# Top-32 attention and capacity routing: the score mask as one comparison on GpSimd, a new order of VectorE's round, transposes issued together

## The chip, the cores and the metric

The kernel runs on one NeuronCore of a Trainium2 chip. Five engines work side by side, each through its own queue in order: TensorE (PE; its weight loads are shown as PEld), VectorE (DVE), ScalarE (ACT), GpSimd (POOL) and SyncE (SP), which issues the DMA transfers here. They wait for each other on semaphores. SBUF holds 128 rows (partitions); PSUM, which TensorE writes, has eight banks of 128 rows by 512 fp32 values. The metric is device time of one execution in microseconds (us); less is better.

## What is computed

Attention over 8 batches, 8 heads, 576 positions and 64 columns, in which each query keeps its 32 largest scores; then a mixture of experts, which routes each of the 4608 rows to its best expert, and in which each expert keeps its 80 rows with the largest gate.

```python
scores = scale * np.matmul(q, k.transpose(0, 1, 3, 2))
kth = np.partition(scores, -top_k, axis=-1)[..., -top_k:-top_k + 1]
mask = scores >= kth
scores = np.where(mask, scores, -1000000000.0)
scores = scores - np.max(scores, axis=-1, keepdims=True)
attn = np.exp(scores)
attn = attn / (np.sum(attn, axis=-1, keepdims=True) + 1e-09)
return np.matmul(attn, v).astype(np.float32)
...
logits = x @ w_gate
expert_idx = np.argmax(logits, axis=1)
...
keep = np.argpartition(-gw, capacity)[:capacity]
...
h = np.maximum(x[tok_idx] @ w1[e], 0.0)
out[tok_idx] = gate_w[tok_idx, None] * (h @ w2[e])
```

All inputs and the output are fp32.

## The kernel before, in words

The attention goes over 32 pairs of heads (`n`: batch and pair). A pair has 576 queries: four blocks of 128 rows and one of 64. In a full block each head is a *unit* of 128 queries by 576 keys; in the last block the 64 rows of both heads together are one unit. So a pair of heads has nine units (`UPP`), and the kernel 288 (`NU`). `run` writes the order out by hand: `step(i)` issues, for each unit, the pieces of work of several units that are in different stages. In the text a step is also called a round, and nine rounds a period; rounds are numbered 0 to 8 by the unit whose first maxima they take.

The stages:

- `load` (SP) brings q, k and v of a pair of heads, `turn` transposes q and k on TensorE into `sp`, a tile of four PSUM banks, of which there is one (`ps_s`), and ScalarE copies them into qT and kT.
- `front` multiplies scores of two units into the same `sp`; ScalarE copies them, scaled, to `s` (L195). A front is issued two rounds before its first unit.
- On VectorE, `parts` takes the eight largest of each of six pieces of a row (L202, "cand"); `search` finds the 24 largest of these by maxima and replacements (L213, L221); ScalarE compares all scores with the 24th and counts (`y`, L218, the sign); VectorE multiplies (L223), takes eight maxima of that (L225), and picks the threshold of the 32nd by the count (L228, `pick`, which writes `thr`).
- `drop` makes the unit's mask (L250): 0 or 1 for "below the threshold", plus the row's largest score, as bf16.
- `turn_w` makes the weights, transposed: TensorE multiplies the masks by `minus` (a diagonal of large negative numbers), which puts them transposed into PSUM (`ab` and `cc`, L268), and adds the transposed scores on top (L272). ScalarE takes the exponential (L275, L276) into `wT`. The `ab` tile has two PSUM banks; `cc` is one bank of a pool of two (`ps_c`).
- `back` multiplies `wT` by v into `cc` (L290), with a column of ones beside v that gives the sums; ScalarE copies the result to `xu` (L292).
- `norm` runs a few rounds behind, a piece a round: it divides by the sums (`z` on GpSimd, reciprocals on VectorE, `xn` on GpSimd, L307), stores `xn`, transposes it through `sp` (L318) into `xT`, and multiplies by the gate's weights (`lp`, L325, in the pool of `cc`); ScalarE copies that to `part` and GpSimd adds it to the logits `lg` (L334). Every two batches `gates` takes the row's best expert.

Three numbers set the order within a round: a letter is a piece of work on VectorE, `back` says how many units behind it works, and `G` is one of the six maxima of the new unit.

```python
back = dict(a=0, b=1, c=1, d=1, e=1, y=2, g=2, h=3, m=3)
for c in "GbGcGdGehGmyGga":
```

Here b to e are the replacements and maxima of `search`, y the multiplication, g the maxima of it, h the pick, m the mask, and a the first maximum over the candidates. After VectorE's letters a round issues `turn_w`, `front` or `turn`, `back` and the pieces of `norm`, each if its unit is due. Stores of zeros into the output (`clear`) and loads of the experts' weights are spread over the periods.

Behind the loop, `judge` checks that every threshold was found (if not, a slower exact path runs the attention again), and `finish` selects the rows of each expert and runs the experts.

## Time and profile before

| | |
|---|---|
| median of 3 runs | 1344.43 us (1344.4 to 1352.03) |
| the profiled execution | 1343.53 us |
| its span, from first to last instruction | 1341.7 us |
| granted TensorE clock, mean | 0.908 |
| VectorE busy | 84% of the span |
| TensorE busy | 81% |
| ScalarE busy | 51% |
| GpSimd busy | 7% |
| the attention loop, as the slices of the page show it | about 20 to 1175 us |

A row of a timeline has the start (us from the span's start), the length, the engine, the line, the operation, "out<-in", the shape and how many instructions are merged in it; in brackets stands how long the engine was idle just before, and what ended that. A row of a table of lines has the count behind an x, then the busy time in us, the mean of one in ns, and the idle time in front of these instructions with its releasers. A row of a table of stretches has the stretch, its length, the busy time and number of instructions of PE, PEld, DVE, ACT and POOL, then the granted clock, the share of the DMA engines and GB/s.

### The profile page before, as it was taken

Reading aid. Unit: us, or ns where it says so; the run is one execution under the profiler, and the core shown is the slowest. Engines: PE = TensorE matmul, PEld = TensorE weight load, DVE = VectorE, ACT = ScalarE, POOL = GpSimd, SP = SyncE. Lnnn points to the kernel's source line nnn. Section 1 sums busy time; section 2 is a strip of 40 time slices with the busy share of each in tenths; the row PEclk is TensorE's granted clock in tenths of the full one; section 3 lists DMA queues with packets and bytes.
Section 4 is the critical chain, followed back from the end, with each engine's and each line's share of the span. In section 5 each row is a group of like instructions: output and inputs, shape, how many; then the busy total and the mean of one; then the engine's idle time right before and its main releaser. Section 6 shows DMA issues by size and latency. Waiting matters only on the chain.

```text
span 1341.7 us, 38270 instructions
## 1 busy us (share of the span) xinstructions
PE 1081.9 (81%) x14862; PEld 834.7 (62%) x14862; DVE 1127.2 (84%) x5383; ACT 679.1 (51%) x1374; POOL 91.8 (7%) x213
## 2 busy tenths in 40 slices
PE   6888888888888888888888888888888888713987
PEld 3666666666666666666666666666666666603887
DVE  5999989999998999999999998999999999585001
ACT  4565555566555556565565556555555565300111
POOL 0000000000000000000000000000000000100111
PEclk9998989999889899898899989898898998855899
DMA  5033322222222122222222211111110110120660
GB/s 142 7 96 100 99 84 69 68 68 69 68 68 56 49 63 64 60 60 59 68 68 69 53 37 37 37 37 33 33 36 21 28 37 11 30 114 5 214 221 24
DMA packets 154590, 85.93 MB, mean 64 GB/s; under 512 B 118304, under 2 KB 136736, under 8 KB 154400
## 3 DMA queue, kind: packets, MB, share of 16 engines
q1 hardware_dynamic: 153376, 80.78, 21.0%
q0 software_dynamic: 1024, 2.62, 0.7%
q8 instruction: 118, 1.93, 0.6%
q14 instruction: 72, 0.59, 0.2%
HBM read 63.19 MB, written 20.19 MB: 62 GB/s over the span
## 4 chain that ended last, share of the span: by engine, by line
PE 47%; DVE 41%; ACT 8%; issue 2%; POOL 0%; DMA 0%; POOLq 0%; DVEq 0%; ACTq 0%
PE sp L190 11%; DVE cand L202 10%; PE ab L272 9%; DVE mask L250 8%; PE cc L290 7%; DVE y L223 6%; DVE w L225 6%; DVE cand L221 4%; PE ab L268 4%; ACT s L195 4%; PE yp L616 3%; PE cc L272 3%; DVE top L213 2%; PE cc L268 2%; PE sp L165 2%
## 5 line engine op out<-in xcount | busy, mean ns | idle before, releaser
L202 DVE MAX8 cand<-s 128x8 f32<-128x96 f32 x1728 | 432.0, 250 | 76.2 <-ACT s L195 76.2
L190 PE MATMUL sp<-kT,qT 64*128 64x288 f32 (+1 forms) x1280 | 233.0, 490 | 48.3 <-ACT s L195 25.7
L275 ACT ACTIVATE wT<-ab 128x1024 f32<-128x1024 f32 (+1 forms) x160 | 150.1, 938 | 236.6 <-PE ab L272 236.6
L290 PEld LDWEIGHTS cc<-vb,wT 128*64 128x64 f32 x4608 | 197.7, 153 | 62.2 <-issue 47.2
L218 ACT ACTIVATE y<-s,w 128x576 f32<-128x576 f32 x288 | 222.9, 774 | 20.2 <-DVE w L213 19.9
L290 PE MATMUL cc<-vb,wT 128*64 128x65 f32 x4608 | 227.2, 241 | 0.0
L195 ACT ACTIVATE s<-sp 128x1152 f32<-128x1152 f32 (+1 forms) x160 | 165.5, 1034 | 112.3 <-PE sp L190 108.0
L223 DVE TENSOR_TENSOR y<-s,y 128x576 f32<-128x576 f32 x288 | 216.6, 752 | 3.4 <-ACT y L218 1.4
L225 DVE MAX8 w<-y 128x8 f32<-128x576 f32 x288 | 214.0, 743 | 0.1
L268 PEld LDWEIGHTS <-mask 128*128 128x128 bf16 (+1 forms) x1600 | 106.2, 101 | 168.2 <-DVE mask L250 122.1
L268 PE MATMUL ab<-minus,mask 128*128 128x128 bf16 (+1 forms) x1280 | 120.1, 216 | 110.0 <-DVE mask L250 106.9
L272 PE MATMUL ab<-qT,kT 64*128 64x128 f32 (+1 forms) x2560 | 193.3, 293 | 0.0
L190 PEld LDWEIGHTS sp<-kT,qT 64*128 64x128 f32 (+1 forms) x1280 | 122.3, 204 | 106.1 <-ACT s L195 44.4
L272 PEld LDWEIGHTS ab<-qT,kT 64*128 64x128 f32 x2560 | 163.6, 196 | 10.0
L250 DVE TENSOR_SCALAR mask<-s,thr,top 128x576 bf16<-128x576 f32 x288 | 166.8, 579 | 1.5 <-DVE cand L202 0.6
L213 DVE MAX8 top<-cand 128x8 f32<-128x48 f32 x576 | 111.3, 193 | 0.1
L221 DVE MATCH_REPLACE8 cand<-top,cand 128x48 f32<-128x48 f32 x576 | 111.3, 193 | 0.0
L290 PE MATMUL cc<-vr,wT 128*64 128x65 f32 x1152 | 97.5, 235 | 0.0
L268 PE MATMUL cc<-minus,mask 128*64 128x128 bf16 (+1 forms) x320 | 76.3, 238 | 0.0
L292 ACT COPY xu<-cc 128x130 f32<-128x130 f32 (+1 forms) x160 | 42.2, 264 | 64.7 <-PE cc L290 64.7
L290 PEld LDWEIGHTS cc<-vr,wT 128*64 128x64 f32 x1152 | 70.4, 151 | 0.0
L272 PE MATMUL cc<-qT,kT 64*64 64x128 f32 (+1 forms) x640 | 69.6, 297 | 0.0
(165 smaller groups left out, 996.1 us busy)
## 6 DMA issues: line engine op xcount, KB each, us to landing
w<-in_moe_w_dram SPq DMA_DIRECT2D x32, 512.0 KB, 4.7
w<-in_moe_w_dram SPq DMA_DIRECT2D x8, 2048.0 KB, 12.9
out_dram<-zero SPq DMA_DIRECT2D x9, 1024.0 KB, 8.2
qn<-in_q_dram SPq DMA_DIRECT2D x64, 128.0 KB, 2.7
kn<-in_k_dram SPq DMA_DIRECT2D x64, 128.0 KB, 2.7
vb<-in_v_dram SPq DMA_DIRECT2D x64, 128.0 KB, 2.4
xd<-xn SPq DMA_DIRECT2D x32, 256.0 KB, 2.4
qn<-in_q_dram SPq DMA_DIRECT2D x32, 32.0 KB, 2.8
```

Source lines behind the costliest of these rows:

```text
L190: nc.tensor.matmul(o, lhsT=qT[d, t * P : t * P + m], rhs=kT[d, j * HS : (j + 1) * HS], start=True, stop=True)
L195: nc.scalar.activation(s[:, : g * S].rearrange("p (j c) -> p j c", c=HS), ps[:, : 2 * g, :HS], Act.Copy, scale=TINY)
L202: nc.vector.max(out=cand[:, j, :], in_=s[:, j * S // NG : (j + 1) * S // NG])
L218: nc.scalar.activation(y, s, Act.Sign, bias=w9[:, 7:8], scale=-1.0, accum_out=cnt)
L221: nc.vector.match_replace(out=cand, in_to_replace=dst, in_values=cand, imm_value=LOW)
L223: nc.vector.tensor_tensor(out=y, in0=s, in1=y, op=Alu.mult)
L225: nc.vector.max(out=w9[:, 8:], in_=y)
L250: nc.vector.tensor_scalar(self.mask[i], s, self.thr[:, i : i + 1], top[:, 0, 0:1], op0=Alu.is_lt, op1=Alu.add)
L268: nc.tensor.matmul(dst[h][c], lhsT=masks[h][:, keys[c]], rhs=eye[h], start=c in (0, NF), stop=False, skip_group_check=True)
L272: nc.tensor.matmul(dst[h][c], lhsT=kT[heads[h], keys[c]], rhs=qT[heads[h], rows], start=False, stop=True, skip_group_check=True)
L275: nc.scalar.activation(wT[:, : 2 * NF, :m], ab.rearrange("p h c r -> p (h c) r")[:, :, :m], Act.Exp, scale=scale)
L290: nc.tensor.matmul(cc[r : r + TL, o], lhsT=wT[:, h * NF + c if c < NF else 2 * NF, r : r + TL], rhs=vb[:, c, h, :] if c < NF else vr[:, h, ...
```

## The change

The mask becomes one comparison, s below thr, without the row's largest score added, and moves from VectorE to GpSimd (`below`). The exponentials then are taken without subtracting the largest score; `z`, the sums, are kept for all pairs in one tile, and `judge` also asks that none of them is below 1e-30. The lean path keeps `drop`.

The round is written anew: the pick of a unit and its mask come a round later than before and stand at the round's start; y stands at its end; `turn_w` and `back` come one round later, so the loop drains in five rounds.

`turn` issues all ten transposes of q and k before the first of ScalarE's two copies. `norm` transposes `xn` into two tiles of the small pool of `cc`, of which the second also takes the product with the gate's weights; that product is done in column halves of 64. The tile of zeros shrinks to 128 columns, and the stores of zeros take rows of 512 bytes from it.

```diff
-    zero = const.tile([P, Dm], F32, name="zero")
+    zero = const.tile([P, P], F32, name="zero")
...
+            self.z = vpool.tile([P, 1 if lean else NP, NK, 2], F32, name="z")
+            nc.gpsimd.memset(self.z, 1.0)
...
-            for j, (src, name) in enumerate(zip(self.qk.pop(n), ("qT", "kT"))):
-                t = self.qkp.tile([P, S], F32, name=name, tag=name)
-                ps = four[:, 2 * j : 2 * j + 2, :].rearrange("p j c -> p (j c)")
-                self.turn_in(ps, src.rearrange("p c h d -> p c (h d)"))
-                nc.scalar.copy(t, ps[:, :S])
-                ts_.append(t)
-            self.turned[n] = ts_
+            ps = [four[:, 2 * j : 2 * j + 2, :].rearrange("p j c -> p (j c)") for j in range(2)]
+            for j, src in enumerate(self.qk.pop(n)):
+                self.turn_in(ps[j], src.rearrange("p c h d -> p c (h d)"))
+            self.turned[n] = [self.qkp.tile([P, S], F32, name=name, tag=name) for name in ("qT", "kT")]
+            for j in range(2):
+                nc.scalar.copy(self.turned[n][j], ps[j][:, :S])
...
-            self.drop(i)
-            yield
+
+        def below(self, i):
+
+            self.top.pop(i)
+            self.mask[i] = self.rows.tile([P, S], BF16, name="mask", tag="mask", bufs=3)
+            nc.gpsimd.tensor_scalar(self.mask[i], self.s.pop(i), self.thr[:, i : i + 1], None, op0=Alu.is_lt)
...
-            while self.fronts:
-                yield
-            ps = self.four()[:, :2, :].rearrange("p j c -> p (j c)")
-            self.turn_in(ps, xn)
+
+            ps, rest = (self.ps_c.tile([P, 512], F32, name="xp", tag="cc") for _ in range(2))
+            for c in range(NF):
+                nc.tensor.transpose(ps[:, c * P : (c + 1) * P], xn[:, c, :], ident)
+            nc.tensor.transpose(rest[:, :TL], xn[:TL, NF, :], ident[:TL, :TL])
             xT = self.xT
-            nc.scalar.copy(xT[:, :S], ps[:, :S])
-            yield
-            ps = self.ps_c.tile([P, 512], F32, name="lp", tag="cc")
-            lp = ps[:, : NK * E].rearrange("p (c e) -> p c e", e=E)
+            nc.scalar.copy(xT[:, : NF * P], ps)
+            nc.scalar.copy(xT[:, NF * P : S], rest[:, :TL])
+            yield
+            lp = rest[:, P : P + NK * E].rearrange("p (c e) -> p c e", e=E)
             for c in range(NK):
-                nc.tensor.matmul(lp[:, c, :], lhsT=xT[:, c * P : (c + 1) * P], rhs=wg[:, hp, :], start=True, stop=True)
+                for r in range(0, P, TL):
+                    nc.tensor.matmul(lp[r : r + TL, c, :], lhsT=xT[:, c * P + r : c * P + r + TL], rhs=wg[:, hp, :],
+                                     start=True, stop=True)
...
-                back = dict(a=0, b=1, c=1, d=1, e=1, y=2, g=2, h=3, m=3)
-                for c in "GbGcGdGehGmyGga":
+                back = dict(a=0, b=1, c=1, d=1, e=1, y=2, g=3, h=4, m=4)
+                for c in "GhmbGcGdGeGGgay":
...
+                    elif c == "m":
+                        if 0 <= i - back[c] < NU:
+                            self.below(i - back[c])
...
-                j = i - 3
+                j = i - 4
...
-                j = i - 4
+                j = i - 5
```

What it does to the order, at three places. Line numbers of the changed kernel run a few higher than those of the kernel before (L202 becomes L204, L213 L215, L221 L223, L223 L225, L225 L227, L228 L230, L268 L274, L290 L296). First VectorE, one round before, from the maximum of the candidates to the maximum of y:

```order
L213 MAX w_6463<-cand 128x8
L228 SCALAR_TENSOR_TENSOR pick,thr<-past,cnt,w_6338 128x9
L202 MAX cand<-s 128x8
L250 TENSOR_SCALAR mask<-s,thr,top 128x576
L223 TENSOR_TENSOR y<-s,y 128x576
L202 MAX cand<-s 128x8
L225 MAX w_6387<-y 128x8
```

And in the changed kernel, the end of one round and the start of the next:

```order
L215 MAX w_6758<-cand 128x8
L204 MAX cand<-s 128x8 x2
L227 MAX w_6645<-y 128x8
L215 MAX top<-cand 128x8
L225 TENSOR_TENSOR y<-s,y 128x576
L204 MAX cand<-s 128x8
L230 SCALAR_TENSOR_TENSOR pick,thr<-past,cnt,w_6645 128x9
```

The mask is gone from VectorE; y stands last in its round, a whole round ahead of the maximum that reads it, and the pick second in the next.

Second GpSimd's queue over one period, before:

```order
L301 TENSOR_SCALAR z<-xu 128x8
L301 TENSOR_SCALAR z<-xu 64x2
L307 TENSOR_TENSOR xn<-xu,z 128x512
L307 TENSOR_TENSOR xn<-xu,z 64x128
L334 TENSOR_TENSOR lg<-lg,part 128x40
```

And in the changed kernel:

```order
L307 TENSOR_SCALAR z<-xu 128x8
L307 TENSOR_SCALAR z<-xu 64x2
L238 TENSOR_SCALAR mask<-s,thr 128x576 x2
L313 TENSOR_TENSOR xn<-xu,z 128x512
L313 TENSOR_TENSOR xn<-xu,z 64x128
L238 TENSOR_SCALAR mask<-s,thr 128x576 x3
L343 TENSOR_TENSOR lg<-lg,part 128x40
L238 TENSOR_SCALAR mask<-s,thr 128x576 x4
```

Nine masks now stand among the pieces of `norm`; the addition to `lg`, which reads what ScalarE copied of TensorE's product, stands between the masks of rounds 1 and 2.

Third TensorE around the transposes of `xn`, with the engines that an instruction waits for, before:

```order
L165 MATMUL sp<-ident,xn 128x128 [waits Activation_49,Pool_49]
L165 MATMUL sp<-ident,xn 128x128 x3
L166 MATMUL sp<-ident,xn 128x64 [waits Pool_49]
L190 MATMUL sp<-kT,qT 128x288 [waits Activation_49]
L190 MATMUL sp<-kT,qT 128x288 x3
L290 MATMUL cc<-vb_128,wT 64x65 x8
```

And in the changed kernel:

```order
L192 MATMUL sp<-kT,qT 128x288 [waits Activation_49]
L192 MATMUL sp<-kT,qT 128x288 x3
L324 MATMUL xp<-ident,xn 128x128 [waits Activation_49]
L324 MATMUL xp<-ident,xn 128x128 x3
L325 MATMUL xp<-ident,xn 128x64 [waits Activation_49]
L296 MATMUL cc<-vb_130,wT 64x65 x8
L296 MATMUL cc<-vr_131,wT 64x65 x2
```

The front no longer stands behind these transposes, but the back does, and the last transpose has a wait of its own for ScalarE: one of the two small buffers still holds the `cc` of the back behind it, so the second tile takes the place of the first.

More of the change, by code (lines that the diff above doesn't have):

```diff
@@ L20 @@
 LOW = -3.0e38
+FAR = 1e-30
 TINY = 2.0 ** -48
@@ L109, in clear @@
         return [lambda i=i: nc.sync.dma_start(
-            out[i : i + r, :].rearrange("(p r) d -> p r d", p=P),
-            zero.unsqueeze(1).to_broadcast([P, r // P, Dm])) for i in range(0, N, r)]
+            out[i : i + r, :].rearrange("(p r) (c d) -> p (r c) d", p=P, d=P),
+            zero.unsqueeze(1).to_broadcast([P, r * Dm // P // P, P])) for i in range(0, N, r)]
     class Attention:
@@ L168, in turn @@
         def turn(self, n):
-            ts_ = []
             four = self.four()
-            for j, (src, name) in enumerate(zip(self.qk.pop(n), ("qT", "kT"))):
-                t = self.qkp.tile([P, S], F32, name=name, tag=name)
-                ps = four[:, 2 * j : 2 * j + 2, :].rearrange("p j c -> p (j c)")
-                self.turn_in(ps, src.rearrange("p c h d -> p c (h d)"))
-                nc.scalar.copy(t, ps[:, :S])
-                ts_.append(t)
-            self.turned[n] = ts_
+            ps = [four[:, 2 * j : 2 * j + 2, :].rearrange("p j c -> p (j c)") for j in range(2)]
[4 more added lines that the diff above has]
+                nc.scalar.copy(self.turned[n][j], ps[j][:, :S])
         def front(self, n, t):
@@ L248, in drop @@
             s, top = self.s.pop(i), self.top.pop(i)
-            self.mask[i] = self.rows.tile([P, S], BF16, name="mask", tag="mask", bufs=3)
+            self.mask[i] = self.rows.tile([P, S], BF16, name="mask", tag="mask", bufs=2)
             nc.vector.tensor_scalar(self.mask[i], s, self.thr[:, i : i + 1], top[:, 0, 0:1], op0=Alu.is_lt, op1=Alu.add)
@@ L298, in norm @@
             parts = ((slice(0, P), slice(0, NF)), (slice(0, TL), slice(NF, NK)))
-            z = self.small.tile([P, NK, 2], F32, name="z", tag="z")
+            z = self.z[:, n % NP if not self.lean else 0]
             for p, cs in parts:
@@ L430, in run @@
                 i = 0
-                while i < NU + 4 or later:
+                while i < NU + 5 or later:
                     step(i)
@@ L438, in judge @@
             small = self.small
-            least = small.tile([P, 1], F32, name="least", bufs=1)
-            nc.vector.tensor_reduce(least, self.thr, axis=AX, op=Alu.min)
+            least = small.tile([P, 2], F32, name="least", bufs=1)
+            nc.vector.tensor_reduce(least[:, 0:1], self.thr, axis=AX, op=Alu.min)
+            nc.vector.tensor_reduce(least[:, 1:2], self.z.rearrange("p n c h -> p (n c h)"), axis=AX, op=Alu.min)
+            nc.vector.tensor_scalar(least[:, 1:2], least[:, 1:2], -FAR, None, op0=Alu.add)
+            nc.vector.tensor_tensor(out=least[:, 0:1], in0=least[:, 0:1], in1=least[:, 1:2], op=Alu.min)
             ps = self.ps_c.tile([P, 512], F32, name="tp", tag="cc")
-            nc.tensor.transpose(ps[:1, :P], least, ident)
+            nc.tensor.transpose(ps[:1, :P], least[:, 0:1], ident)
             low = small.tile([1, 1], F32, name="low", bufs=1)
```

## The prediction

> **What bounds the kernel now.** I read the page's busy times first, then the chain that ended last, then the stretch from 200 to 1100 us, where the attention loop runs undisturbed, by lines, and at last the timeline of one pair of heads.
>
> ```profile
> PE 1081.9 (81%) x14862; PEld 834.7 (62%) x14862; DVE 1127.2 (84%) x5383; ACT 679.1 (51%) x1374; POOL 91.8 (7%) x213
> ...
> PE 47%; DVE 41%; ACT 8%; issue 2%; POOL 0%; DMA 0%; POOLq 0%; DVEq 0%; ACTq 0%
> ...
> 200.00:1100.00 900.00, 758.80 (x9906) 573.80 (x9902) 835.10 (x4134) 522.59 (x1058) 56.37 (x131) 0.93 0.20 53
> ...
> L202 DVE MAX8 cand<-s 128x8 f32<-128x96 f32 x1354 | 338.9, 250 | 55.8 <-ACT s L195 55.8
> ...
> L250 DVE TENSOR_SCALAR mask<-s,thr,top 128x576 bf16<-128x576 f32 x225 | 130.3, 579 | 0.6 <-PE ab L272 0.3 <-DVE cand L202 0.3
> ```
>
> VectorE is busy for 835 of these 900 us, and almost all of its rest (55.8) is waiting for fresh scores s. The chain nevertheless runs through TensorE for 47%: the loop is one in which VectorE makes masks, TensorE turns them into weights and, behind them in its queue, makes the scores that VectorE needs next. 225 masks in 900 us are 4.0 us a unit, and a pair of heads is nine units: 36.0 us a period, 32 periods.
>
> **VectorE's part.** One unit's round on VectorE, from one first maximum to the next:
>
> ```profile
> 605.73 0.24 DVE L202 MAX8 cand<-s 128x8 f32<-128x96 f32 x1
> ...
> 606.94 0.21 DVE L228 SCALAR_TENSOR_TENSOR pick<-past,cnt,w 128x9 f32<-128x9 f32 x1
> 607.07 0.08 DVE L228 DVE_READ_ACCUMULATOR pick<-past,cnt,w 128x1 f32 x1
> ...
> 607.26 0.58 DVE L250 TENSOR_SCALAR mask<-s,thr,top 128x576 bf16<-128x576 f32 x1
> 607.76 0.75 DVE L223 TENSOR_TENSOR y<-s,y 128x576 f32<-128x576 f32 x1
> 608.43 0.26 DVE L202 MAX8 cand<-s 128x8 f32<-128x96 f32 x1
> ...
> 609.37 0.24 DVE L202 MAX8 cand<-s 128x8 f32<-128x96 f32 x1
> ```
>
> A round without waits is 609.37 - 605.73 = 3.64 us. The mask holds the queue for 607.76 - 607.26 = 0.50 us, so the new round is 3.14 us: 28.3 us for nine instead of 32.8. If VectorE alone counted, this would be 4.5 us a period. It doesn't, so the rest of the loop has to be walked through.
>
> **The mask on GpSimd.** No row shows this form there. The nearest:
>
> ```profile
> L307 POOL TENSOR_TENSOR xn<-xu,z 128x512 f32<-128x512 f32 x32 | 33.4, 1043 | 89.2 <-DVE z L304 84.6 <-PE cc L290 4.5
> ...
> L334 POOL TENSOR_TENSOR lg<-lg,part 128x40 f32<-128x40 f32 x24 | 8.6, 360 | 403.6 <-ACT part L333 403.6
> ...
> L74 POOL MEMSET R<- 128x640 f32 x1 | 0.6, 621 | 0.0
> ```
>
> From below: a memset of 640 takes 0.62, so 576 elements 0.56 us, without reading anything. From above: the product of 512 with two inputs grows by (1043 - 360) / 472 = 1.45 ns an element, so 576 take 1.14 us. I take 1.0, by the product, the nearest row of arithmetic on a full tile, less a little for its second input. In the new round the pick stands second, so it ends 0.37 us into the round; with about 0.13 us to start, the mask is ready 1.5 us into it. At 607.84 it was ready 2.1 us into the old, longer round. The Trainium skill (GPSIMD Engine Reference, its opening) speaks against the move: it calls this engine the wrong one for ordinary elementwise arithmetic, VectorE being about twice as fast. Twice the 579 ns would be 1.16 us, and the sum by it about 1225; no row here shows the move itself.
>
> **TensorE's part, and ScalarE's behind it.** Durations as start to start, at full clock but for the three rows from 623 to 628:
>
> ```profile
> 604.26 0.40 PE L268 MATMUL ab<-minus,mask 128*128 128x128 bf16 x4 [1.58 <-DVE mask L250]
> ...
> 606.12 1.14 PE L190 MATMUL sp<-kT,qT 64*64 64x288 f32 x8
> 608.01 1.24 PE L190 MATMUL sp<-kT,qT 64*128 64x288 f32 x8 [0.75 <-ACT s L195]
> 609.18 0.69 PE L290 MATMUL cc<-vb,wT 128*64 128x65 f32 x16
> ...
> 610.50 0.40 PE L268 MATMUL ab<-minus,mask 128*128 128x128 bf16 x4
> ...
> 613.50 0.66 PE L165 MATMUL sp<-ident,xn 128*128 128x128 f32 x4
> ...
> 617.58 1.28 PE L325 MATMUL lp<-wg,xT 128*128 128x8 f32 x10
> 618.72 0.38 PE L268 MATMUL ab<-minus,mask 128*128 128x128 bf16 x4
> ...
> 622.90 0.29 PE L268 MATMUL ab<-minus,mask 128*128 128x64 bf16 x4 [1.67 <-DVE mask L250]
> ...
> 623.65 1.97 PE L272 MATMUL ab<-qT,kT 64*128 64x64 f32 x16
> ...
> 625.96 2.29 PE L190 MATMUL sp<-kT,qT 64*128 64x288 f32 x8
> ...
> 632.39 0.66 PE L165 MATMUL sp<-ident,kn 128*128 128x128 f32 x4 [1.03 <-ACT qT L176]
> ...
> 633.17 0.68 PE L290 MATMUL cc<-vb,wT 128*64 128x65 f32 x8
> ...
> 634.49 0.40 PE L268 MATMUL ab<-minus,mask 128*128 128x128 bf16 x4
> ...
> 636.95 1.24 PE L190 MATMUL sp<-kT,qT 64*128 64x288 f32 x8
> ```
>
> ```profile
> 609.29 1.13 ACT L195 ACTIVATE s<-sp 128x1152 f32<-128x1152 f32 x1 [0.59 <-PE sp L190]
> ...
> 610.77 0.78 ACT L218 ACTIVATE y<-s,w 128x576 f32<-128x576 f32 x1
> ...
> 613.25 1.02 ACT L275 ACTIVATE wT<-ab 128x1024 f32<-128x1024 f32 x1 [1.61 <-PE ab L272]
> 614.18 0.27 ACT L276 ACTIVATE wT<-cc 128x128 f32<-128x128 f32 x1
> 614.40 0.64 ACT L320 COPY xT<-sp 128x576 f32<-128x576 f32 x1
> ```
>
> So a whole turn_w takes 2.46 (634.49 to 636.95), and 1.86 from its second mask on (604.26 to 606.12); a front 1.17 (608.01 to 609.18), the short one 1.14; a back 1.32 (609.18 to 610.50; the short one too, 633.17 to 634.49); the short turn_w 0.75 and then 2.31 at half clock, 1.15 at full; one set of transposes about 0.8 (632.39 to 633.17); lp 1.14 (617.58 to 618.72). On ScalarE the exponentials take 1.15 (613.25 to 614.40) and s 1.13.
>
> What the other edits do here. The transposes of q and k lose the 1.03 us in which TensorE stood for the copy of q, once a period. The wait for the copies then falls on the next front, which a back now stands in front of. The transposes of xn no longer hold the large buffer, but the second small one comes free only when ScalarE has copied the first, so the fifth transpose, and the back queued behind it, waits for that copy, and the copy for s. lp becomes twice as many products of half the columns: from below 20 passes at back's 1.32 / 40 each, 0.66; from above 2.28, as many passes again at the old price. I take 0.7, since back's halves are the same kind.
>
> **One period, walked through** (us from the start of round 0, in which the third pair of the head before is turned):
> - Mask ready 1.5; second half of turn_w 3.4; front 4.55; exponentials 4.55 and s 5.7, in time for round 2 at 6.28. Four transposes 5.15; ScalarE's copy, after s, 6.3; last transpose 6.5; back 7.8; lp 8.5; ScalarE's part 8.75.
> - Now GpSimd's queue: lg stands in it ahead of round 2's mask. Its input comes at 8.75, it ends at 9.25, and the mask, whose pick was done at 6.65, is ready only at 10.3.
> - Second half of turn_w 12.2; front 13.35; s 14.5. Round 4 was due at 12.56: VectorE stands 1.95 us.
> - Short turn_w 15.25; transposes of q and k 16.9; the two copies 18.2, back beside them 18.2; front 19.4; s 20.6, due 14.5 + 6.28 = 20.8.
> - Short back 20.7; turn_w 23.2; short front 24.3; back 25.6; turn_w 28.1; front 29.25; s 30.45, due 14.5 + 15.7 = 30.2.
>
> The period is 30.45 us where lg is issued (three of four periods). Without lg, round 2's turn_w starts when lp ends, at 8.5, and s comes at 13.35: 29.25. Mean 30.15. The old period holds 36.0 - 32.8 (nine rounds) - 2.2 (55.8 of waiting for s in 25 periods) = 1.0 us of reciprocals, gates and short waits; I add half of that, 0.5, since some of it falls where VectorE waits for s.
>
> **The clock.** One thing is left:
>
> ```profile
> 620.10:623.50 3.40, 1.73 (x28) 1.23 (x26) 3.37 (x20) 2.01 (x4) 0.00 (x0) 1.00 0.00 0
> 623.50:626.90 3.40, 3.40 (x27) 2.97 (x27) 3.33 (x21) 0.71 (x2) 0.30 (x1) 0.51 0.00 0
> ```
>
> After a stretch in which TensorE was busy for half the time, it is granted half the clock. The mean of 0.93 says that this holds for 14% of the time, 5 us a period. In the new loop TensorE is on the path nearly throughout, so the same 5 us would cost 2.5; but its gaps are shorter (1.2 for the xn copy, 1.1 for the late mask). I take half, 1.25, between 0 and 2.5.
>
> **The sum.** 30.15 + 0.5 + 1.25 = 31.9 us, 4.1 less than 36.0; times 32, 131 us. At the end come a fifth step of draining and three small VectorE instructions, some 2.5 us. The zero fill in 512-byte rows costs nothing: DMA's share is 0.20, and nobody waits for these stores. From the profiled execution's 1343.53 us (span 1341.7), which is within 0.1% of the median 1344.43: 1343.5 - 131 + 2.5 = 1215 us.
>
> The ends: no half clock, -40; mask 0.56, twice in a period on the path, -28: 1147. Full half clock +40; mask 1.14, +9; ScalarE's queue (a sign of 0.78 us ahead of s or wT) and port conflicts, 1 us a period, +32: 1296.
>
> **Sharing between VectorE and GpSimd.**
>
> ```profile
> 1141.34 1.39 POOL L307 TENSOR_TENSOR xn<-xu,z 128x512 f32<-128x512 f32 x2 [4.46 <-PE cc L290]
> ...
> 1142.08 0.25 DVE L202 MAX8 cand<-s 128x8 f32<-128x96 f32 x1
> ...
> 1142.36 0.39 DVE L228 SCALAR_TENSOR_TENSOR pick<-past,cnt,w 128x9 f32<-128x9 f32 x1
> ```
>
> Here a pick, which has two inputs, took 0.39 instead of 0.21 and ended when GpSimd's xn ended (1142.73); a one-input maximum beside the same xn kept its 0.25. A mask at 0.5 to 1.5 of a round lies beside one-input work; y comes at 2.45. The Trainium skill (SBUF — State Buffer, "Who interferes with whom") has the rule for it: VectorE's two-input instructions and a GpSimd instruction that reads exclude each other wholly. The row agrees. By it the late mask of round 2 holds the pick of round 3 by up to 0.9 us, which the wait for s at round 4 covers.
>
> **Rivals.**
> - VectorE alone bounds (buffers hide all of the walk): 28.3 + 0.5 = 28.8, 7.2 us less a period, about 1115. Against it stand lg in GpSimd's queue and the copy in the middle of the transposes. 0.07.
> - TensorE and ScalarE give back more (half clock as before, y in front of s): 34.3 us a period, about 1290 and up to 1330. 0.17.
> - No effect, because the walk, not VectorE, already set the period: within 1%, 1344. Against it: VectorE was busy for 93% of the loop, so what it loses can't all have been slack. 0.05.
> - Slower: a GpSimd mask of m us ends at 0.5 + m; past m = 1.95 it holds y, and the round is 0.5 + m + 0.67. It decides from 4.0, m = 2.85. At m = 3.2 it is 4.37 a unit, 39.3 a period, 32 x 3.3 = 106 more: 1450. Only a compare three times as dear as xn's product does this. 0.05.
>
> Forecast 0.66. Range 1160 to 1285. About 1% is what a measurement of this kernel tells from no change: faster by more 0.90, within 0.05, slower 0.05.
>
> **What would show it.** Right: VectorE without L250, rounds of 3.14; masks on POOL near 1.0 us; POOL's lg waiting on ScalarE with the mask behind it, VectorE idle for s about 2 us a period in front of round 4; TensorE's fifth xn transpose waiting for xT; no TensorE wait for qT. Wrong: masks past 1.2 us, y or picks lengthened in most rounds, a granted clock well under 0.9 in the loop, or a period under 30.

## The result, and the profile after

| | before | after |
|---|---|---|
| median of 4 runs | 1345.61 us (1344.4 to 1352.03) | 1307.79 us (1299.17 to 1308.85) |
| ratio, with its 95% interval | 1 | 0.970 (0.964 to 0.975) |
| profiled execution's span | 1341.7 us | 1307.1 us |
| granted TensorE clock, mean | 0.908 | 0.900 |

The change gains 38 us. The forecast was 1215 us, a gain of 129; its range ended at 1285. The direction was right, the size was not. One of the four runs of the kernel with the old transposes, below, was in a slow state, 1346.43 us, and is not counted.

The page of the changed kernel, first the busy times, then the chain that ended last, then four groups of instructions (count, busy us, mean ns, and the idle time in front with its releaser):

```profile
PE 1064.4 (81%) x15182; PEld 816.9 (62%) x15182; DVE 1000.7 (77%) x5098; ACT 676.6 (52%) x1406; POOL 612.1 (47%) x502
...
DVE 43%; PE 34%; POOL 9%; issue 7%; ACT 5%; DMA 0%; SPq 0%; POOLq 0%; ACTq 0%; DVEq 0%
...
L238 POOL TENSOR_SCALAR mask<-s,thr 128x576 bf16<-128x576 f32 x288 | 495.8, 1723 | 394.9 <-DVE cand L223 386.8
L204 DVE MAX8 cand<-s 128x8 f32<-128x96 f32 x1728 | 399.1, 245 | 163.2 <-ACT s L197 162.9
...
L225 DVE TENSOR_TENSOR y<-s,y 128x576 f32<-128x576 f32 x288 | 236.0, 819 | 7.6 <-ACT y L220 7.6
...
L274 PE MATMUL ab<-minus,mask 128*128 128x128 bf16 (+1 forms) x1280 | 125.4, 223 | 128.3 <-POOL mask L238 127.7
```

The same two waits in the kernel before:

```profile
L202 DVE MAX8 cand<-s 128x8 f32<-128x96 f32 x1728 | 432.0, 250 | 76.2 <-ACT s L195 76.2
...
L268 PE MATMUL ab<-minus,mask 128*128 128x128 bf16 (+1 forms) x1280 | 120.1, 216 | 110.0 <-DVE mask L250 106.9
```

VectorE lost its masks: it is busy for 127 us less. Most of that came back as waiting. It now waits 162.9 us for scores (76.2 before), and TensorE stands 127.7 us in front of products that read a mask (106.9 before). One mask takes 1.723 us on GpSimd, where the forecast had 1.0. POOL, which was not on the chain before, is 9% of it.

How long a period is can be read from GpSimd, which makes one xn for each pair of heads. Its timeline in the kernel before, the first and the last xn:

```profile
64.60 1.39 POOL L307 TENSOR_TENSOR xn<-xu,z 128x512 f32<-128x512 f32 x2 [2.50 <-DVE z L304]
...
1167.56 1.39 POOL L307 TENSOR_TENSOR xn<-xu,z 128x512 f32<-128x512 f32 x2
```

And in the changed kernel, with the masks and the addition to lg of one period between:

```profile
64.97 1.91 POOL L313 TENSOR_TENSOR xn<-xu,z 128x512 f32<-128x512 f32 x2
...
656.60 1.91 POOL L313 TENSOR_TENSOR xn<-xu,z 128x512 f32<-128x512 f32 x2
...
661.88 1.72 POOL L238 TENSOR_SCALAR mask<-s,thr 128x576 bf16<-128x576 f32 x1 [1.39 <-DVE cand L223]
...
671.07 0.39 POOL L343 TENSOR_TENSOR lg<-lg,part 128x40 f32<-128x40 f32 x1 [4.35 <-ACT part L342]
671.45 3.42 POOL L238 TENSOR_SCALAR mask<-s,thr 128x576 bf16<-128x576 f32 x2
...
1136.13 1.39 POOL L313 TENSOR_TENSOR xn<-xu,z 128x512 f32<-128x512 f32 x2
```

Between first and last lie 31 periods: 1102.96 / 31 = 35.58 us before, 1071.16 / 31 = 34.55 us after. The period shrank by 1.0 us; the forecast had it shrink by 4.1, from 36.0 to 31.9. (The last period drains and is shorter, so the means lie a little under the undisturbed stretch.) Before the first xn and behind the last the kernels differ by 3 us together, so the loop holds nearly all of the gain, and all of what is missing.

The 31 periods are not alike. By the starts of xn, the eight without an addition to lg took 30.8 to 33.2 us, 31.7 on average; those with it, leaving out the draining last one, took 32.9 to 40.3, 36.0 on average. The walk's sum gave 31.0 (29.25 + 0.5 + 1.25) and 32.2: without lg it was nearly right, and what is missing lies in the periods with lg.

One period with lg, from round 0 at 661.30, on VectorE's timeline:

```profile
656.78 1.48 DVE L225 TENSOR_TENSOR y<-s,y 128x576 f32<-128x576 f32 x1
...
661.30 0.25 DVE L204 MAX8 cand<-s 128x8 f32<-128x96 f32 x1
661.47 0.21 DVE L230 SCALAR_TENSOR_TENSOR pick<-past,cnt,w 128x9 f32<-128x9 f32 x1
...
664.42 0.25 DVE L204 MAX8 cand<-s 128x8 f32<-128x96 f32 x1
...
668.31 0.21 DVE L230 SCALAR_TENSOR_TENSOR pick<-past,cnt,w 128x9 f32<-128x9 f32 x1
...
673.73 0.77 DVE L225 TENSOR_TENSOR y<-s,y 128x576 f32<-128x576 f32 x1
...
680.12 0.26 DVE L204 MAX8 cand<-s 128x8 f32<-128x96 f32 x1 [5.62 <-ACT s L197]
...
696.93 0.25 DVE L204 MAX8 cand<-s 128x8 f32<-128x96 f32 x1
```

The period is 696.93 - 661.30 = 35.63 us, and one wait in it, 5.62 us in front of round 4, is most of the lost time. Followed back: round 2's pick ended at 668.52, but its mask ran only from 671.45 to 673.17, behind lg, which began at 671.07. The same stretch on TensorE:

```profile
668.63 0.27 PE L325 MATMUL xp<-ident,xn 64*128 64x64 f32 x1 [1.18 <-ACT xT L327]
...
670.04 0.71 PE L333 MATMUL xp<-wg,xT 128*64 128x8 f32 x20
670.68 0.40 PE L274 MATMUL ab<-minus,mask 128*128 128x128 bf16 x4
...
673.22 0.51 PE L274 MATMUL ab<-minus,mask 128*128 128x128 bf16 x4 [1.97 <-POOL mask L238]
...
676.53 2.29 PE L192 MATMUL sp<-kT,qT 64*128 64x288 f32 x8
```

TensorE stood 1.97 us between its first and its second mask. The front behind it, which makes the scores that VectorE waits for, began at 676.53 and took 2.29 us; at full clock it takes 1.24. The table of stretches (PE, PEld, DVE, ACT, POOL busy, then the granted clock) shows why:

```profile
669.95:673.36 3.41, 1.44 (x38) 1.18 (x34) 3.41 (x18) 1.23 (x4) 2.29 (x3) 1.00 0.29 113
673.36:676.78 3.42, 3.42 (x27) 2.55 (x27) 1.13 (x3) 0.75 (x1) 1.50 (x1) 0.50 0.02 5
676.78:680.19 3.41, 3.41 (x22) 2.07 (x24) 0.07 (x1) 1.68 (x4) 0.00 (x0) 0.50 0.00 0
```

In the stretch of the stand TensorE was busy for 1.44 of 3.41 us, 42%, and for the next two stretches it was granted half the clock, just where the path runs through it. A stand as long in round 0 of the same period, 1.95 us up to 663.66, lay across two stretches, which were still busy for 59% and 84%, and the clock stayed at 1.00 behind both.

### The profile page after: what moved, and what is told of

It is laid out like the page before. It is cut to its first block, busy times and chain, and to the rows that moved or that the text cites. A ratio compares the mean times of both kernels' runs of the same rounds, so it can differ in the third digit from the quotient of the medians.

```text
span 1307.1 us, 38981 instructions
## 1 busy us (share of the span) xinstructions
PE 1064.4 (81%) x15182; PEld 816.9 (62%) x15182; DVE 1000.7 (77%) x5098; ACT 676.6 (52%) x1406; POOL 612.1 (47%) x502
## 4 chain that ended last, share of the span: by engine, by line
DVE 43%; PE 34%; POOL 9%; issue 7%; ACT 5%; DMA 0%; SPq 0%; POOLq 0%; ACTq 0%; DVEq 0%
DVE cand L204 12%; DVE y L225 9%; POOL mask L238 8%; DVE w L227 7%; PE ab L278 7%; PE sp L192 7%; DVE cand L223 5%; ACT s L197 4%; PE cc L296 3%; PE yp L631 3%; PE ab L274 3%; DVE top L215 3%; PE cc L278 2%; DVE pick L230 2%; DVE top L506 1%
## 5 line engine op out<-in xcount | busy, mean ns | idle before, releaser
L238 POOL TENSOR_SCALAR mask<-s,thr 128x576 bf16<-128x576 f32 x288 | 495.8, 1723 | 394.9 <-DVE cand L223 386.8
L204 DVE MAX8 cand<-s 128x8 f32<-128x96 f32 x1728 | 399.1, 245 | 163.2 <-ACT s L197 162.9
L225 DVE TENSOR_TENSOR y<-s,y 128x576 f32<-128x576 f32 x288 | 236.0, 819 | 7.6 <-ACT y L220 7.6
L274 PEld LDWEIGHTS <-mask 128*128 128x128 bf16 (+1 forms) x1600 | 106.4, 102 | 200.8 <-POOL mask L238 140.5
L274 PE MATMUL ab<-minus,mask 128*128 128x128 bf16 (+1 forms) x1280 | 125.4, 223 | 128.3 <-POOL mask L238 127.7
L192 PE MATMUL sp<-kT,qT 64*128 64x288 f32 (+1 forms) x1280 | 223.1, 473 | 5.0 <-ACT kT L180 2.5
L278 PE MATMUL ab<-qT,kT 64*128 64x128 f32 (+1 forms) x2560 | 213.2, 314 | 0.0
L227 DVE MAX8 w<-y 128x8 f32<-128x576 f32 x288 | 213.1, 740 | 0.0
L296 PEld LDWEIGHTS cc<-vb,wT 128*64 128x64 f32 x4608 | 180.0, 141 | 45.9 <-ACT wT L282 26.7
L296 PE MATMUL cc<-vb,wT 128*64 128x65 f32 x4608 | 207.7, 228 | 0.9 <-ACT wT L282 0.9
L278 PEld LDWEIGHTS ab<-qT,kT 64*128 64x128 f32 x2560 | 180.7, 214 | 11.0
L215 DVE MAX8 top<-cand 128x8 f32<-128x48 f32 x576 | 109.5, 190 | 0.1
L223 DVE MATCH_REPLACE8 cand<-top,cand 128x48 f32<-128x48 f32 x576 | 109.4, 190 | 0.0
L296 PE MATMUL cc<-vr,wT 128*64 128x65 f32 x1152 | 92.8, 225 | 0.0
L274 PE MATMUL cc<-minus,mask 128*64 128x128 bf16 (+1 forms) x320 | 78.3, 245 | 0.0
L278 PE MATMUL cc<-qT,kT 64*64 64x128 f32 (+1 forms) x640 | 75.7, 319 | 0.0
L296 PEld LDWEIGHTS cc<-vr,wT 128*64 128x64 f32 x1152 | 65.6, 141 | 0.0
L343 POOL TENSOR_TENSOR lg<-lg,part 128x40 f32<-128x40 f32 x24 | 9.2, 383 | 113.5 <-ACT part L342 113.5
```

The source lines that it names most:

```text
L192: nc.tensor.matmul(o, lhsT=qT[d, t * P : t * P + m], rhs=kT[d, j * HS : (j + 1) * HS], start=True, stop=True)
L204: nc.vector.max(out=cand[:, j, :], in_=s[:, j * S // NG : (j + 1) * S // NG])
L223: nc.vector.match_replace(out=cand, in_to_replace=dst, in_values=cand, imm_value=LOW)
L225: nc.vector.tensor_tensor(out=y, in0=s, in1=y, op=Alu.mult)
L227: nc.vector.max(out=w9[:, 8:], in_=y)
L238: nc.gpsimd.tensor_scalar(self.mask[i], self.s.pop(i), self.thr[:, i : i + 1], None, op0=Alu.is_lt)
```

## The experiments

The theory after the result: lg's place in GpSimd's queue and a mask 0.72 us dearer than assumed make TensorE stand long enough in front of round 2's second mask that its clock is halved, and the late scores cost more than the mask itself. Rivals: the mask's length or place hardly matters, and VectorE and GpSimd holding each other, the fifth transpose of xn, or TensorE's own work sets the period.

**The addition to lg behind the mask** (e1_lg_late).

```diff
                 nc.scalar.copy(part, lp)
+                yield
                 nc.gpsimd.tensor_tensor(out=lg, in0=lg, in1=part, op=Alu.add)
```

> The addition to lg is issued one round later, behind the mask of round 2 in GpSimd's queue. Theory A (the late mask of round 2 sets the period): in the changed kernel's trace the pick of that round ended at 668.53 but its mask ran from 671.45 to 673.17, behind lg, and TensorE stood and was then granted half the clock until 678.8. Without lg ahead, the mask is ready at about 670.4, before lp ends at 670.75, so turn_w starts 2.5 us sooner and mostly at full clock: 2.5 to 4.4 us in 24 of 32 periods, 60 to 105 us: 1203 to 1248 us. Theory B (the length of the mask, 1.72 us, or the clock alone sets the period, and another wait takes its place): less than 15 us, 1293 to 1308.

Measured: 1199.83 us, ratio to the kernel before 0.889 (0.886 to 0.891). One yield is worth 108 us against the changed kernel. GpSimd's timeline at round 2, in this kernel:

```profile
648.47 1.72 POOL L238 TENSOR_SCALAR mask<-s,thr 128x576 bf16<-128x576 f32 x1 [2.00 <-DVE cand L223]
650.83 0.40 POOL L344 TENSOR_TENSOR lg<-lg,part 128x40 f32<-128x40 f32 x1 [0.63 <-ACT part L342]
```

and two groups of its page:

```profile
L204 DVE MAX8 cand<-s 128x8 f32<-128x96 f32 x1728 | 398.6, 244 | 78.6 <-ACT s L197 78.5
...
L274 PE MATMUL ab<-minus,mask 128*128 128x128 bf16 (+1 forms) x1280 | 121.0, 217 | 83.6 <-POOL mask L238 82.8
```

The mask of round 2 is out 0.64 us before lg begins. VectorE's wait for scores halves, from 162.9 to 78.5. The mask costs what it did, 1.72 us, so this run tells lg's place from the mask's price. It is somewhat faster than expected.

**The mask back on VectorE, all else as changed** (e2_mask_dve).

```diff
-            nc.gpsimd.tensor_scalar(self.mask[i], self.s.pop(i), self.thr[:, i : i + 1], None, op0=Alu.is_lt)
+            nc.vector.tensor_scalar(self.mask[i], self.s.pop(i), self.thr[:, i : i + 1], None, op0=Alu.is_lt)
```

> Only the engine of the mask is undone: the same single comparison at the same place of the round, on VectorE. Theory A (the move to GpSimd is what costs: 1.72 us a mask on the path twice a period, its queue behind lg, y held by xn): VectorE's round goes back to 3.64 us, 33.3 a period with reciprocals and gates, the mask is ready 1.0 us into the round, and TensorE's walk fits into that; 35.1 becomes 33.3 to 34: 1250 to 1275 us, faster than the changed kernel. Theory B (the move is what gains: 0.50 us of VectorE a unit): 0.50 x 288 = 144 us come back, less the old waits: 1340 us or more, no faster than before.

Measured: 1306.56 us, 0.968 (0.966 to 0.970). Neither number came. The stretch from 200 to 1050 us, and by lines in it:

```profile
200.00:1050.00 850.00, 718.61 (x9888) 540.54 (x9886) 822.72 (x4036) 508.63 (x1052) 60.76 (x128) 0.93 0.21 56
```

```profile
L204 DVE MAX8 cand<-s 128x8 f32<-128x96 f32 x1321 | 306.8, 246 | 1.4 <-ACT s L197 1.4
...
L238 DVE TENSOR_SCALAR mask<-s,thr 128x576 bf16<-128x576 f32 x220 | 129.3, 588 | 24.4 <-DVE pick L230 0.9
```

VectorE is busy for 822.72 of 850 us, and waits for scores for 1.4. So the rest of the change alone gives about the same 39 us, up to VectorE's bound, and moving the mask added nothing to it as it was placed: GpSimd's late masks took back about what VectorE was relieved of. Against the run with lg out of the way the move is worth 1306.6 - 1199.8 = 107 us, if lg's place is of no account while VectorE makes the masks; that was not run.

**The fifth transpose of xn a round later** (e3_tail_late). This takes TensorE's wait for ScalarE's copy (35.2 us in all in the changed kernel) out of round 0.

```diff
-            ps, rest = (self.ps_c.tile([P, 512], F32, name="xp", tag="cc") for _ in range(2))
+            ps = self.ps_c.tile([P, 512], F32, name="xp", tag="cc")
...
             nc.scalar.copy(xT[:, : NF * P], ps)
             yield
+            rest = self.ps_c.tile([P, 512], F32, name="xp", tag="cc")
+            nc.tensor.transpose(rest[:, :TL], xn[:TL, NF, :], ident[:TL, :TL])
+            nc.scalar.copy(xT[:, NF * P : S], rest[:, :TL])
```

> Only the last transpose of xn (and its copy) is issued one round later, behind the back, so that TensorE does not stand for ScalarE's copy. Theory A (this wait, 42.9 us of the weight loads over 31 periods, is on the path to lp, lg and the mask of round 2): TensorE gains 1.15 us in front of the back and gives about 0.5 back in front of lp: 15 to 25 us, 1283 to 1293. Theory B (the wait is covered, or returns whole in front of lp): 1300 to 1312.

Measured: 1320.36 us, 0.977 (0.973 to 0.982): some 13 us slower than the changed kernel, with an interval that overlaps its by a little, and so not faster. The wait at the fifth transpose is gone and 20.5 of its 35.2 us are back in front of lp, so lp is about 0.3 us earlier. What became of that, on GpSimd and on VectorE at the same time:

```profile
675.14 0.72 POOL L344 TENSOR_TENSOR lg<-lg,part 128x40 f32<-128x40 f32 x1 [4.02 <-DVE top L215]
```

```profile
675.00 0.74 DVE L225 TENSOR_TENSOR y<-s,y 128x576 f32<-128x576 f32 x1
```

lg now meets VectorE's y and takes 0.72 us instead of 0.39 (688 ns on average over the run, against 383); it ends 0.12 us after y. The mask behind it starts 6.45 us after the start of the mask before (675.85 - 669.40), and in the changed kernel it was 6.45 as well (671.45 - 665.00). TensorE, which comes earlier, only stands longer for it, 2.30 us instead of 1.97, and the mean clock is 0.888. So taking this wait away gains nothing here: what TensorE gains ahead of that stand is lost in it. What it would be worth if lg did not meet y, this run can't tell.

**What GpSimd's forms cost alone** (e5_forms; a single run). The kernel with eighteen GpSimd instructions on tiles of the mask's size behind its end.

```diff
+                nc.gpsimd.tensor_scalar(fb, fo, slot[:, 0:1], None, op0=Alu.is_lt)
+                nc.gpsimd.tensor_scalar(ff, fo, slot[:, 0:1], None, op0=Alu.is_lt)
+                nc.gpsimd.tensor_scalar(fb[:, :288], fo[:, :288], slot[:, 0:1], None, op0=Alu.is_lt)
+                nc.gpsimd.tensor_scalar(fb, fo, 2.0, None, op0=Alu.is_lt)
+                nc.gpsimd.tensor_scalar(ff, fo, 2.0, None, op0=Alu.add)
+                nc.gpsimd.tensor_tensor(out=ff, in0=fo, in1=fo, op=Alu.add)
```

> The changed kernel, with 18 GpSimd instructions on spare tiles behind the last expert, three times each of: the mask's form (576 columns, fp32 to bf16, is_lt against a column); the same to fp32; the same over 288 columns; is_lt against a constant; an addition of a constant to fp32; an addition of two tiles to fp32. Theory A (a comparison, or writing bf16, is dear here): the mask's form takes 1.7 us alone too, and addition of a constant under 1.1. Theory B (the length comes from sharing with VectorE): alone, the mask's form takes 1.0 to 1.15 us. The time of the whole is 15 to 30 us above the changed kernel's.

It took 1329.12 us. Its timeline on GpSimd, where nothing else works (the lines in the order of the diff, behind a memset):

```profile
1296.48 0.59 POOL L669 MEMSET hot<- 128x576 f32 x1
1297.18 1.74 POOL L671 TENSOR_SCALAR sel<-hot,slot 128x576 bf16<-128x576 f32 x1
1298.91 1.71 POOL L672 TENSOR_SCALAR hot<-hot,slot 128x576 f32<-128x576 f32 x1
1300.61 0.99 POOL L673 TENSOR_SCALAR sel<-hot,slot 128x288 bf16<-128x288 f32 x1
1301.69 1.66 POOL L674 TENSOR_SCALAR sel<-hot 128x576 bf16<-128x576 f32 x1
1303.31 1.68 POOL L675 TENSOR_SCALAR hot<-hot 128x576 f32<-128x576 f32 x1
1305.07 1.15 POOL L676 TENSOR_TENSOR hot<-hot 128x576 f32<-128x576 f32 x1
```

The mask's form takes 1.74 us alone too, so nothing that ran beside it made it dear. Neither the comparison (the addition takes 1.68), nor bf16 (1.71 without), nor the threshold's column (1.66 with a constant) is the reason: a TENSOR_SCALAR, one tensor in, is half as dear again as a TENSOR_TENSOR, two inputs (here the same tile twice), at 1.15. So the mask's form is as dear alone, as the first theory had it, but the addition is not under 1.1, and why the form is dear stays open. The prediction's 1.14 us for a two-input product of 576 elements agrees with the addition's 1.15; it was the wrong row. The Trainium skill (GPSIMD Engine Reference, 4.1 Engine selection) says the opposite: on GpSimd two-input work is about twice as slow as on VectorE and one-input work roughly at line rate. The measurement decides: 1723 ns against VectorE's 588 for the same comparison (with the mask back on VectorE) is three times, and the two-input form, 1.15 us against 0.74 for VectorE's y, is one and a half times.

**The transposes of q and k as before** (e4_old_turn).

```diff
-            for j, src in enumerate(self.qk.pop(n)):
-                self.turn_in(ps[j], src.rearrange("p c h d -> p c (h d)"))
...
-            for j in range(2):
-                nc.scalar.copy(self.turned[n][j], ps[j][:, :S])
+            for j, (src, name) in enumerate(zip(self.qk.pop(n), ("qT", "kT"))):
...
+                self.turn_in(ps, src.rearrange("p c h d -> p c (h d)"))
+                nc.scalar.copy(t, ps[:, :S])
```

> Only turn is undone: q's transposes, q's copy, k's transposes, k's copy, as before. Theory A (the prediction's step: TensorE's stand for q's copy comes back, 1.0 us a period, in front of a front that is on the path): 25 to 33 us over the changed kernel, 1325 to 1340. Theory B (TensorE waits for the late mask of round 2 anyway, and the stand is covered): within 8 us of it, 1300 to 1316.

Measured: 1329.61 us, the median of three runs (1325.92 to 1341.21), 0.989 (0.981 to 0.997), some 22 us slower than the changed kernel. The group of k's transposes there, which waited 0.5 us in all in the changed kernel:

```profile
L169 PE MATMUL sp<-ident,kn 128*128 128x128 f32 x128 | 24.3, 320 | 23.3 <-ACT qT L180 23.3
```

The copy's wait is back, 23.3 / 32 = 0.7 us a period, and so is its price: 22 / 32 = 0.7, below the 1.03 that the prediction counted. It is uncertain by some 0.3, as the runs lie 18 to 33 us above the changed kernel. The second theory, within 8 us, fell; without this part the change would have gained some 15 us instead of 38.

**Half a mask** (e6_half_mask), and **half a mask with lg late** (e7_lg_half). The comparison runs over 288 columns, at 1.00 us, the price that the prediction assumed.

```diff
-            nc.gpsimd.tensor_scalar(self.mask[i], self.s.pop(i), self.thr[:, i : i + 1], None, op0=Alu.is_lt)
+            nc.gpsimd.tensor_scalar(self.mask[i], self.s.pop(i)[:, :HS], self.thr[:, i : i + 1], None, op0=Alu.is_lt)
...
-                    nc.tensor.matmul(dst[h][c], lhsT=masks[h][:, keys[c]], rhs=eye[h], start=c in (0, NF), stop=False,
+                    nc.tensor.matmul(dst[h][c], lhsT=masks[h][:, keys[c if self.lean else c % 2 if c < NF else 0]][:, : P if c < NF else TL], rhs=eye[h], start=c in (0, NF), stop=False,
```

> The mask is compared over the first 288 columns only, and TensorE reads the first two blocks of it twice, so the same products run on a mask of 1.00 us instead of 1.72; the comparison of the other columns is left out, the selection is not the reference's. lg stays ahead of the mask of round 2. Theory A (the mask's length is the term that the prediction had wrong; with the 1.0 us it assumed, its sum should come true): 1205 to 1235. Theory B (the queue behind lg and the half clock after it cost most): the mask's 0.72 us, twice in a period, is 40 us: 1255 to 1275.

> Both: lg one round later, and the mask over 288 columns (1.00 us; the comparison of the other columns is left out). With lg out of the way a period took 30.2 us in the trace, with TensorE standing for the mask in rounds 0 and 7. Theory A (mask length still on the path): 0.7 to 1.1 us a period, 22 to 35 us: 1165 to 1178. Theory B (TensorE's own work and VectorE's round are the bound by now): within 10 us of 1200.

Measured: 1193.44 us, 0.883 (0.880 to 0.887), and 1140.26 us, 0.846 (0.843 to 0.849). Two groups of the first one's page:

```profile
L204 DVE MAX8 cand<-s 128x8 f32<-128x96 f32 x1728 | 400.8, 246 | 86.8 <-ACT s L197 86.3
L238 POOL TENSOR_SCALAR mask<-s,thr 128x288 bf16<-128x288 f32 x288 | 287.8, 1001 | 489.9 <-DVE cand L223 476.4
```

With the mask at 1.0 us and lg still ahead of it the period is 31.0 us, by the starts of xn, where the prediction had 31.9. TensorE's stand in front of round 2's second mask is 1.37 us instead of 1.97, and half clock follows it in 9 of the 24 periods with lg, instead of 21. So 0.72 us of mask carries 114 us, and moving lg 108; both together give 168, less than their sum: each alone already raises the mean clock from 0.900 to 0.949 and 0.948, and both together raise it only to 0.966. Both runs came out below what either theory expected. In these, VectorE's y is back at 740 ns, since xn has nearly ended when y begins.

**TensorE kept busy through the stand** (e8_fill). Ten products of the unit matrix, into columns of cc that nothing reads, between the two masks of round 2. Their starts in cc's bank change what cc accumulates.

```diff
             for h in range(2):
+                if h == 1 and t == NF - 1 and not self.lean and (n - 1) % HP:
+                    for _ in range(10):
+                        nc.tensor.matmul(cc[:, 384:512], lhsT=ident, rhs=ident, start=True, stop=True, skip_group_check=True)
```

> The changed kernel, and ten products of the unit matrix into unused columns of cc, between the first and the second mask of the turn_w of round 2, in the periods that have lg: TensorE works through 1.65 us of its 2.4 us stand. Theory A (the stand costs mostly by the half clock that follows it: scores 2.70 instead of 1.53 and front 2.29 instead of 1.24 in the trace): 2.2 us in up to 24 periods come back, 40 to 53 us: 1255 to 1268. Theory B (the clock follows something else, or the lateness of the mask alone counts): within 8 us of 1307, or slower by the added work.

Measured: 1274.46 us, 0.945 (0.941 to 0.949), 33 us faster than the changed kernel with 480 more matmul records. Stretches around round 2, and TensorE's timeline there:

```profile
653.40:656.80 3.40, 3.40 (x74) 3.21 (x71) 3.40 (x21) 2.03 (x7) 1.44 (x2) 1.00 0.44 168
656.80:660.20 3.40, 3.40 (x40) 2.88 (x40) 1.99 (x7) 0.69 (x1) 2.35 (x2) 1.00 0.02 5
```

```profile
655.48 2.50 PE L275 MATMUL cc<-ident 128*128 128x128 f32 x20
657.81 0.39 PE L277 MATMUL ab<-minus,mask 128*128 128x128 bf16 x4
...
659.76 1.24 PE L192 MATMUL sp<-kT,qT 64*128 64x288 f32 x8
```

The mask is as late as in the changed kernel (655.74 to 657.46 here), but the clock stays at 1.00 and the front takes 1.24 instead of 2.29. So it is in all 22 periods in which the trace has this front as one row; in the changed kernel, with a stand of 1.97 us in nearly all of them, it took 2.29 in ten of 22 and 1.24 to 1.71 in the others. This shows the half clock by itself: here it is a consequence of the stand, and taking it away is worth 33 us. The whole of it may be worth more, since the filling ends 0.35 us behind the mask, and since half clock still comes elsewhere, behind the stand in round 0 (782.99 to 786.40, for one, after a stretch busy for 51%). By the mean grants, 0.900 over 1307 us and 0.939 over 1273, the time at half clock fell from 261 to 155 us. The expected 40 to 53 us was somewhat too much.

**turn_w and back one round later** (e9_turnw_late_lg with lg late, e10_turnw_late without).

```diff
-            self.mask[i] = self.rows.tile([P, S], BF16, name="mask", tag="mask", bufs=3)
+            self.mask[i] = self.rows.tile([P, S], BF16, name="mask", tag="mask", bufs=4)
...
-                    if t == 1 and h == 0 and n + 1 < NP:
+                    if t == 2 and h == 0 and n + 1 < NP:
                         due.append(n + 1)
...
-                j = i - 4
+                j = i - 5
                 if 0 <= j < NU and units[j][2]:
                     self.turn_w(*units[j][:2])
...
-                j = i - 5
+                j = i - 6
                 if 0 <= j < NU and units[j][2]:
                     self.back(*units[j][:2])
```

> turn_w and back of a unit come one round later (turn of the next pair one unit later too, a fourth mask buffer, single buffers for lg and part), and GpSimd adds to lg one round later. Theory A (what is left over in the run with lg late, 1200 us, is TensorE standing for masks that come late in their own round, with the next front queued behind: 82.8 us there, and 78.5 us of VectorE waiting for s): with a whole round of slack for every mask the stand falls under 20 us and the wait for s under 40, so 1200 - 80 with 20 us either way, 1120 to 1165, and rounds of VectorE near 3.2 us. Theory B (what is left is TensorE's own work and ScalarE's behind it, or VectorE's and GpSimd's two-input work holding each other): no change, 1190 to 1215.

> The same without the later addition to lg: turn_w and back one round later, lg still ahead of round 2's mask. Theory A (the 1.72 us mask and lg cost time only through TensorE's stand in front of the second mask, and the half clock that follows it): the late mask of round 2 now has a round to spare, so nearly the same time as its companion, 1125 to 1175, and no half clock at round 2. Theory B (lg's place or the length of the mask costs by itself, whatever TensorE's order): 1270 to 1308, as the changed kernel.

Measured: 1155.91 us, 0.860 (0.857 to 0.863), and 1156.16 us, 0.859 (0.856 to 0.863): the same. Of the second one, GpSimd at round 2, and two groups of its page:

```profile
649.45 0.27 POOL L343 TENSOR_TENSOR lg<-lg,part 128x40 f32<-128x40 f32 x1 [2.46 <-ACT part L342]
649.70 3.57 POOL L238 TENSOR_SCALAR mask<-s,thr 128x576 bf16<-128x576 f32 x2
```

```profile
L204 DVE MAX8 cand<-s 128x8 f32<-128x96 f32 x1728 | 419.9, 260 | 35.1 <-ACT s L197 35.0
...
L274 PE MATMUL ab<-minus,mask 128*128 128x128 bf16 (+1 forms) x1280 | 120.2, 216 | 25.2 <-ACT wT L281 24.4
```

lg still stands ahead of the mask and the mask still takes 1.72 us, but TensorE no longer waits for it: what is left of its 25.2 us ends with ScalarE's wT. This takes lg's place and the mask's length off the path together, as the theory said. In the period shown there is no half clock at round 2. It is not gone from the loop: in other periods it follows the short turn_w (804.30 to 807.71, for one, after a stretch in which TensorE was busy for 78%). Of the kernels that leave nothing out these two are the fastest, at 14% less time than before. The period of the second one is (986.57 - 64.53) / 31 = 29.7 us by the starts of xn.

## Why the prediction missed

**The step that failed** is "The mask on GpSimd": 1.0 us, between 0.56 and 1.14. It is 1.72, outside both bounds. Its own sign of being wrong, "masks past 1.2 us", came. Both bounds came from rows of other forms, a memset and a two-input product, and the prediction took the two-input one as an upper bound, "less a little for its second input". On this engine the one-input form is the dearer one, 1.74 us alone against 1.15. The remark that only a compare "three times as dear as xn's product" would make the kernel slower put the danger at m = 2.85, by a mask that holds y in VectorE's queue. No mask does that here: y at 673.73 lies wholly beside the mask that runs to 674.87 and takes 0.77 us instead of 0.74. The mask did harm far below that length, through TensorE.

**How 0.72 us became 3.4.** The walk's own steps hold up to the scores, with this mask in them. The period above, with lg, against the walk's 30.45 + 0.5 + 1.25 = 32.2 us:

- Round 0's mask ended 2.3 us into the period (661.88 + 1.72 - 661.30) instead of 1.5, and lg began at 9.77 instead of 8.75. Round 2's mask, behind it, was ready at 11.87 instead of 10.3: twice 0.72, and 0.13 of smaller parts.
- From there to s the walk had 4.2 us (10.3 to 14.5), and it took 6.95 (11.87 to 18.82): 2.75 more. That is the half clock. The prediction gave it 1.25 us a period, a flat half of what it had been, and argued that "its gaps are shorter", with 1.1 for the late mask. The gap was 1.97, and the halved stretch fell on the scores and the front, the only path to s.
- The rest of the period took 16.81 us instead of 15.95: five of VectorE's rounds at 3.12, 0.73 in which y is held by xn once, a wait for s of 0.26, and reciprocals. The sum's 0.5 covers part of the difference; y beside xn it had only in its upper end, as port conflicts.

32.2 + 1.57 + (2.75 - 1.25) + (0.86 - 0.5) = 35.6, the measured 35.63. So two of the sum's terms were wrong, and the second hung on the first: the clock was priced as a flat half of what it had been, though it is the mask that makes the stand. The runs show the dependence: with a mask of 1.0 us the time is 1193, a little below the forecast; with a stand that is filled, 33 us of it come back.

**What was right.** VectorE's round is 664.42 - 661.30 = 3.12 us (forecast 3.14). lg stands ahead of round 2's mask and waits for ScalarE's part, and VectorE waits for scores in front of round 4; a run with only lg moved gives 108 us. lp in halves takes 0.71 us (0.7). The fifth transpose waits 1.18 us for xT (1.2). The wait for qT is gone, 0.5 us in all, and undoing it costs some 22 us. The exclusion between VectorE's two-input work and GpSimd's appears where y meets xn, which has two inputs itself: 1.48 us instead of 0.74. The prediction expected it beside the masks too, with a pick held by up to 0.9 us; that was wrong. Besides the y above, in the last run a pick that begins at 651.14, inside the mask from 649.70, takes 0.20 us.

**The rivals.** The time lies where "TensorE and ScalarE give back more" put it, 1290 to 1330, and half of its mechanism is what happened: the half clock as before. The other half, a sign y in front of s on ScalarE, is not what delays s here. "VectorE alone", 1115 us, was given 0.07 because of lg's place and the copy amid the transposes; with a round's slack for the masks the kernel comes to 1156. Outside the loop the kernel became some 3 us shorter instead of 2.5 longer; the cause stays open.

**What stays open.** In the last two runs VectorE's candidate maxima take 260 ns on average instead of 245, 21 us in all, in stretches in which all its instructions are longer. No run here tells why.

## What to carry to other kernels

An operation that moves to another engine has the price of its own form there: where the trace has no such row, the nearest row need not be a bound (it was none here), and a run with a few such instructions behind the end of the kernel settles it. Before work is put into a queue, look at what stands ahead of it there and who is queued behind the engine that waits; a consumer one stage later cost a fourth mask buffer here and made both the dear mask and its place harmless. And a gap on TensorE isn't priced by its length alone: the same 1.97 us had half clock behind it in most periods and not in all. Ask which work would run at half clock behind it.

## What the runs showed of the hardware

- GpSimd on 128x576: one-input TENSOR_SCALAR 1.66 to 1.74 us, two-input TENSOR_TENSOR 1.15, memset 0.59; 288 columns of the mask 0.99, so about (1.74 - 0.99) / 288 = 2.6 ns an element.
- TensorE's grant fell to 0.50 for two stretches of 3.41 us after one in which it was busy for 42% and stood for 1.97 us at a time; filled, it stayed at 1.00. The Trainium skill (TensorE: Matmul & The Clock Gate, Part 1) names at least one idle window of about 3.4 us as the condition for half rate. The measurement decides: a window that was not idle was enough here. The one ahead of half clock was busy for 42% here, 51% in the kernel before (620.10 to 623.50), and 78% in the last run (800.88 to 804.30). Busy share alone doesn't decide it: in the changed kernel a stretch busy for 49% (833.80 to 837.21) kept the full clock behind it.
- GpSimd's xn, with two inputs, and VectorE's two-input y exclude each other: y takes 1.48 us instead of 0.74. GpSimd's one-input mask doesn't hold y, which takes 0.77 beside it.
